# Order of small work beside a dense TensorE stream: key sums, kv, h split and query products, in linear attention with a gated feed-forward layer

## The chip, the cores and the metric

The kernel runs on one core of a Trainium2 chip. The metric is the device time of one execution in microseconds, the median of several runs. The engines are named as the profile names them: PE (TensorE matmuls), PEld (its weight loads), DVE (VectorE), ACT (ScalarE), POOL (GpSimd) and SP (SyncE, which here only issues DMAs).

## The reference

Linear attention over 8 batches, 8 heads, 576 tokens and 64 columns, then a gated feed-forward layer over all 4608 tokens:

```python
q_s = softmax(q, axis=-1)             # over the 64 columns
k_s = softmax(k, axis=2)              # over the 576 tokens
kv  = einsum('bhsd,bhse->bhde', k_s, v)
x   = einsum('bhsd,bhde->bhse', q_s, kv)      # then (4608, 512)
gate = sigmoid(x @ w_gate)            # (512, 1536)
out  = (gate * (x @ w_val)) @ w_out   # (1536, 512)
```

## The kernel before

**Blocks and steps.** The 4608 tokens are worked through in 9 blocks w of T = 512 (NW = 9). A block has NS = 6 steps, `at` 0 to 5; a step takes two of the twelve slices of 128 columns of the hidden width. Block 0 has code of its own beside the preparation of the weights, and its 12 slices are done by about 180 us. From block 1 on the main loop (lines 1061 to 1083) writes each step's work in one fixed order; each engine executes its own part of it in that order.

**A step.** `g1` (line 651) multiplies the block's x by w_gate and w_val in a Strassen-like scheme of seven products, each of 12 matmuls with 256 columns (L661), into three PSUM tiles y, z, rr. All operands are split into a high and a low fp32r part, and a product is hi x hi + hi x lo + lo x hi. Every product's result is moved to the SBUF tile `sg` by ACT (L679, L681, L684, L689) or added to it by DVE (L687, L693); ACT takes the sigmoids (L694, L697, L698), DVE multiplies gate and value (L700 to L702). The first product goes to y, the second to z, and the third adds to y, so it can't start before L679 has copied y away. `h_split` (line 706) then makes the high and low parts of h from `sg` on DVE (L711, L712). `g2` (line 720) multiplies the h of the step before by w_out in 24 matmuls of 512 columns (L729), so it lags g1 by one step. In step 0 that closes the block before, and `acc_out` copies its four results with ACT (L635) and sends them.

**The next block beside it.** `side_a` and `side_b` put the attention of block w + 1 into the steps of block w; `load_next` fetches what block w + 2 needs. By step:

- 0: DVE takes the maxima of q (natural layout) and subtracts them; the first two key tiles have their maxima subtracted.
- 1: the other three key tiles; ACT takes exp of q (L461), of the five key tiles (L361) and the last two of the four key sums (`k_sum`, L317: an exp over transposed keys whose sum is kept); DVE sums q.
- 2: PE multiplies keys by values (`k_mm`, L382, 40 matmuls of 128 columns); DVE subtracts the maxima from the transposed q (`qT_sub`, L493), which needs the qT and q_b transfers; `k_done` then divides kv by the key sums on DVE (L392) and splits it (ACT L416, DVE L417).
- 3 and 4: exp, scaling and split of the transposed q.
- 4: `x_mm` (line 532) multiplies q by kv (L542), and `x_ev` moves the result; `c_subs` builds Strassen sums, into ring tiles.
- 5: after g1, `c_split` splits the seven operands that the next block's g1 takes (ACT L600, DVE L601), then h_split follows. Their order is B11, T1, T2, B21, T3, B22, T4, which is also the order in which g1's products use them.

Batches of 576 and blocks of 512 don't match: a block of queries mostly has two parts that belong to two batches (`x_parts`), of 128 and 384 columns for block 2, then 192 and 320, 256 and 256, 320 and 192, 384 and 128, 448 and 64; block 8 has one part. `x_mm` multiplies each part by hi x hi, hi x lo and lo x hi of its batch's kv.

All transfers of q, k and v stand in SP's queue in program order. The `ring` pool of 11 buffers holds q and key tiles, the splits of q and the sums of c_subs in turn.

Of the kernel before, what the change touches and what calls it, by code (L numbers as in the profile page):

```python
# [21 lines left out]
T = 512  # L22
# [6 lines left out]
NS = NJ // 2  # L29
# [23 lines left out]
def attn_moe(ctx: ExitStack, tc: tile.TileContext, qf, qn, qT, k, kT, v, wg, wv, wo, out):  # L53
# [28 lines left out]
    kv_sb = const.tile([P, 2, 2, NP, P], F32R, name="kv_sb")  # L82
# [232 lines left out]
    def k_sum(b, hp):  # L315
        t = kT_sb.pop((b, hp))
        nc.scalar.activation(  # L317
            t, t, AF.Exp, bias=kneg[b][:, hp:hp + 1], accum_out=ksum[b][:, hp:hp + 1]
        )
# [33 lines left out]
    def k_sub(b, t, eng=nc.vector):  # L353
        n = KTILES[t][1]
        kt = kt_sb[b, t]
        eng.tensor_tensor(out=kt[:n], in0=kt[:n], in1=kmb[b][:n], op=ALU.subtract)

    def k_exp(b, t):
        n = KTILES[t][1]
        kt = kt_sb[b, t]  # L360
        nc.scalar.activation(kt[:n], kt[:n], AF.Exp)  # L361
# [13 lines left out]
    def k_mm(b, t):  # L375
        n = KTILES[t][1]
        kt, vt = kt_sb[b, t], v_sb[b, t]
        if t == 0:
            kvps[b] = ps_at.tile([P, NP, P], F32, name="at")
        for hp in range(NP):  # L380
            sl = slice(hp * P, (hp + 1) * P)
            nc.tensor.matmul(  # L382
                kvps[b][:, hp], lhsT=kt[:n, sl], rhs=vt[:n, sl],
                start=(t == 0 and hp == 0), stop=(t == len(KTILES) - 1 and hp == NP - 1),
                skip_group_check=True,
            )

    def diag_put(o, ps, k_r, h0, h1):

        for a in range(2):  # L390
            sl = slice(a * D, (a + 1) * D)
            nc.vector.tensor_tensor(  # L392
                out=o(sl), in0=ps[sl, :, sl],
                in1=k_r[sl, h0:h1].unsqueeze(2).broadcast_to([D, h1 - h0, D]), op=ALU.mult,
            )
# [8 lines left out]
    def k_done(b):  # L404
        k_r = ksum.pop(b)
        nc.vector.tensor_scalar_add(k_r, k_r, EPS)
        nc.vector.reciprocal(k_r, k_r)
        kv = kmax_b[:, 0:NP * D].rearrange("p (h e) -> p h e", e=D)
        diag_put(lambda sl: kv[sl], kvps.pop(b), k_r, 0, NP)
        kv_split(b, lambda sl: kv[sl])  # L410

    def kv_split(b, kv):
        hi, lo = (kv_sb[:, b % 2, i] for i in range(2))
        for a in range(2):
            sl = slice(a * D, (a + 1) * D)
            nc.scalar.copy(out=hi[sl, :, sl], in_=kv(sl))  # L416
            nc.vector.tensor_tensor(  # L417
                out=lo[sl, :, sl], in0=kv(sl), in1=hi[sl, :, sl].bitcast(F32), op=ALU.subtract
            )
# [19 lines left out]
    def qn_send(w, what):  # L439
        t = (q_m if what == "m" else q_r)[w]  # L440
        row = dpool.tile([H * T], F32, name=f"q_{what}_row")
        nc.sync.dma_start(
            out=row.rearrange("(p i) -> p i", p=P), in_=t.rearrange("p i one -> p (i one)")
        )
        q_row[w, what] = row.rearrange("(h t) -> h t", t=T)

    def qn_max(w, c):
        if c == 0:
            q_m[w] = const.tile([P, NC * TI, 1], F32, name="q_m")
        nc.vector.tensor_reduce(  # L450
            out=q_m[w][:, c * TI:(c + 1) * TI], in_=qn_sb[w, c], axis=AX.X, op=ALU.max
        )

    def qn_sub(w, c, eng=nc.vector):
        t = qn_sb[w, c]
        m = q_m[w][:, c * TI:(c + 1) * TI]
        eng.tensor_tensor(out=t, in0=t, in1=m.broadcast_to([P, TI, D]), op=ALU.subtract)

    def qn_exp(w, c):
        t = qn_sb[w, c]  # L460
        nc.scalar.activation(t, t, AF.Exp)  # L461
# [29 lines left out]
    def qT_sub(w, hp, eng=nc.vector):  # L491
        t = qT_sb[w, hp]
        eng.tensor_tensor(out=t, in0=t, in1=q_b.pop((w, "m", hp)), op=ALU.subtract)  # L493
# [12 lines left out]
    def qT_exp(w, hp):  # L506
        t = qT_sb[w, hp]
        nc.scalar.activation(t, t, AF.Exp)
# [15 lines left out]
    def x_parts(w):  # L524
        t0 = w * T
        b0, b1 = t0 // S, (t0 + T - 1) // S
        if b0 == b1:
            return [(b0, 0, T)]
        cut = b1 * S - t0
        return [(b0, 0, cut), (b1, cut, T)]  # L530

    def x_mm(w, hp):
        qh, ql = qT_hl.pop((w, hp))
        if w > 1 and hp < 3:
            ps = ps_gv.tile([P, T], F32, name="gv")
        else:
            ps = ps_at.tile([P, T], F32, name="at")
        x_ps[w, hp] = ps
        for b, f, t in x_parts(w):
            kh, kl = (kv_sb[:, b % 2, i, hp] for i in range(2))  # L540
            for lh, rh in ((0, qh), (0, ql), (1, qh)):
                nc.tensor.matmul(  # L542
                    ps[:, f:t], lhsT=kl if lh else kh, rhs=rh[:, f:t],
                    start=(lh == 0 and rh is qh), stop=(lh == 1),
                )

    def x_ev(w, hp):
# [26 lines left out]
    def quarter(kh, th):  # L574
        return x_32[:, 2 * kh:2 * kh + 2, th * HT:(th + 1) * HT]
# [15 lines left out]
    def c_split(i):  # L591
        if i == B11:
            t = bpool.tile([P, 1, 2, 2, HT], F32R, name="c_hl", tag="b")
            c_hl[i] = t[:, 0]
        elif i in C_PAIRS:
            t = cpool.tile([P, 2, 2, 2, HT], F32R, name="c_hl", tag=f"c{list(C_PAIRS).index(i)}")
            c_hl[i], c_hl[C_PAIRS[i]] = t[:, 0], t[:, 1]
        src = c_32.pop(i) if i in c_32 else quarter(*{B11: (0, 0), B21: (1, 0), B22: (1, 1)}[i])
        hi, lo = (c_hl[i][:, x] for x in range(2))
        nc.scalar.copy(out=hi, in_=src)  # L600
        nc.vector.tensor_tensor(out=lo, in0=src, in1=hi.bitcast(F32), op=ALU.subtract)  # L601
# [104 lines left out]
    def h_split(w, p):  # L706
        h_hl[w, p] = hi, lo = [
            two.tile([P, 2, T], F32R, name="h", tag=f"h_{x}") for x in ("hi", "lo")
        ]
        hi, lo = (t.rearrange("p i (q t) -> p (i q) t", q=2) for t in (hi, lo))  # L710
        nc.vector.tensor_copy(out=hi, in_=sg[:, :, 0])  # L711
        nc.vector.tensor_tensor(  # L712
            out=lo, in0=sg[:, :, 0], in1=hi.bitcast(F32), op=ALU.subtract
        )


    def step(w, i):
        return (i - 1) % NS if w == 1 else i
# [20 lines left out]
    def side_a(n, p):  # L739

        b = n if n < B else None
        if p == 0:
            for c in range(NC):
                qn_max(n, c)
            qn_send(n, "m")
            for c in range(NC):
                qn_sub(n, c)
            if b is not None:
                k_sub(b, 0); k_sub(b, 1)
        if p == 1:  # L750
            if b is not None:
                for t in range(2, 5):
                    k_sub(b, t)
            for c in range(NC):
                qn_exp(n, c)
            if b is not None:
                for t in range(5):
                    k_exp(b, t)
                k_sum(b, 2); k_sum(b, 3)
            for c in range(NC):  # L760
                qn_sum(n, c)
        if p == 2:
            if b is not None:
                for t in range(5):
                    k_mm(b, t)
            for hp in range(NP):
                qT_sub(n, hp)
            if b is not None:
                k_done(b)
        if p == 3:  # L770
            for hp in range(NP):
                qT_exp(n, hp)
        if p == 4:
            for hp in range(NP):
                qT_split(n, hp)
# [57 lines left out]
    def after_first(j):  # L833
# [28 lines left out]
        if 6 <= j <= 9:  # L862
            x_mm(1, j - 6)
# [76 lines left out]
    ps = ps_acc.tile([P, DM], F32, name="acc")  # L940
# [116 lines left out]
    def wo_next(w, at):  # L1057
        wo_load(w, step(w, at))

    prev = None  # L1060
    for w in range(1, NW):
        last = w == NW - 1
        for at in range(NS):
            p = step(w, at)
            end = last and at == NS - 1
            g1(w, p, None if end else step(w + (at + 1) // NS, (at + 1) % NS))
            if at == NS - 1 and not last:
                for i in range(7):
                    c_split(i)
            h_split(w, p)  # L1070
            if not last:
                side_a(w + 1, at)
            if prev is None:
                g2_0(NJ - 1)
                wo_next(1, 0)
                wo_next(1, 1)
            else:
                g2(*prev)
                if not end:
                    wo_next(w + (at + 1) // NS, (at + 1) % NS)  # L1080
            prev = (w, at)
            if not last:
                side_b(w + 1, at)
# [39 lines left out]
```

## Time and profile before

| | us |
|---|---|
| median of three runs | 983.6 |
| the other runs | 982.94, 3356.91 |
| the profiled execution | 980.61 |
| its span, first to last instruction | 978.8 |

The profile is of one execution. Times in it count from the span's start. A product of PE overlaps the next one's, so rows give it a duration (0.28 us for 256 columns) longer than the distance between two of them. In the timeline a number in brackets is how long the engine sat idle before the row, and what ended that.

### The profile page before, as it was taken

What the parts mean: (1) busy time and instruction counts of PE and PEld (TensorE: products, weight loads), DVE (VectorE), ACT (ScalarE), POOL (GpSimd) and SP (SyncE); (2) the same over time, 40 slices, a digit from 0 to 9 for tenths busy, and PEclk for the clock granted to TensorE, in tenths of its full rate; (3) what the DMA queues carried; (4) which work ended last, traced back from release to release, by engine and by line L of the source; (5) the groups of instructions that cost most, each with busy time, mean ns of one, the idle gap of its engine ahead of it and who ended that gap; (6) DMA issues with size and microseconds to landing.
All of it is one profiled execution on the core that took longest, in us unless ns stands there. A gap on an engine that the chain in (4) does not pass through costs nothing.

```text
span 978.8 us, 15635 instructions
## 1 busy us (share of the span) xinstructions
PE 947.4 (97%) x6062; PEld 817.1 (83%) x6062; DVE 612.9 (63%) x1013; ACT 471.5 (48%) x812; POOL 167.2 (17%) x316
## 2 busy tenths in 40 slices
PE   5899998999999999999999999999999999999998
PEld 4444543799999999999989999899998999999997
DVE  7788878766566666656675568457644656473242
ACT  4689784563446343625462545253434434443222
POOL 0110001221112111211211111121212121212210
PEclk7999999899999999999999999999999999999999
DMA  9976475899699968997899779997998779868672
GB/s 330 342 273 254 185 274 205 288 350 317 200 269 340 312 203 251 353 296 248 207 379 300 245 160 373 316 270 143 364 315 238 215 238 313 241 181 258 200 215 77
DMA packets 93864, 257.78 MB, mean 263 GB/s; under 512 B 15264, under 2 KB 17568, under 8 KB 93024
## 3 DMA queue, kind: packets, MB, share of 16 engines
q0 software_dynamic: 43712, 168.32, 57.0%
q1 hardware_dynamic: 50080, 88.48, 31.0%
q8 instruction: 48, 0.79, 0.4%
q14 instruction: 24, 0.20, 0.1%
HBM read 228.20 MB, written 28.56 MB: 262 GB/s over the span
## 4 chain that ended last, share of the span: by engine, by line
PE 62%; DMA 20%; issue 6%; DVE 5%; ACT 5%; SPq 1%; POOL 0%; DVEq 0%; POOLq 0%; ACTq 0%
PE gv L661 38%; PE acc L729 20%; DMA ring<-k_in 5%; DMA q_m_row<-q_m 4%; DMA q_b<-q_m_row 3%; DMA ring<-qT_in 2%; PE gv L542 2%; PE at L382 1%; DMA wo_raw<-wo_in 1%; DMA ring<-qf_in 1%; PE acc L643 1%; DMA sg<-wv_in 1%; DMA lent<-v_in 1%; DMA out<-x 1%; ACT ring L461 1%
## 5 line engine op out<-in xcount | busy, mean ns | idle before, releaser
L661 PE MATMUL gv<-c_hl,s_sb 128*128 128x256 f32 x2304 | 286.6, 279 | 5.6 <-ACT sg L679 5.5
L661 PEld LDWEIGHTS gv<-c_hl,s_sb 128*128 128x128 f32 x2304 | 275.2, 188 | 8.2 <-ACT sg L679 7.8
L729 PE MATMUL acc<-wo_hl,h 128*128 128x512 f32 x1152 | 272.2, 392 | 0.0
L729 PEld LDWEIGHTS acc<-wo_hl,h 128*128 128x128 f32 x1152 | 212.9, 188 | 44.4
L661 PE MATMUL gv<-c_hl,a_w 128*128 128x256 f32 x1728 | 224.6, 279 | 0.0
L661 PEld LDWEIGHTS gv<-c_hl,a_w 128*128 128x128 f32 x1728 | 213.8, 188 | 4.3 <-issue 1.0
L282 POOL DMA_DIRECT2D s_sb<-s x188 | 100.1, 532 | 321.0 <-PE gv L661 320.0
L687 DVE TENSOR_TENSOR sg<-gv,sg 128x512 f32<-128x512 f32 x48 | 33.2, 692 | 161.4 <-PE gv L661 161.4
L238 POOL DMA_DIRECT2D wo_hl<-wo x96 | 50.9, 531 | 297.3 <-PE acc L729 297.2
L689 ACT COPY sg<-gv 128x512 f32<-128x512 f32 x48 | 28.1, 586 | 105.5 <-PE gv L661 105.5
L616 PE MATMUL gv<-x,f_w 128*128 128x512 f32 x160 | 72.4, 606 | 3.6 <-ACT h L624 3.5
L679 ACT COPY sg<-gv 128x512 f32<-128x512 f32 x48 | 28.0, 583 | 88.8 <-PE gv L661 64.5
L691 DVE TENSOR_TENSOR sg<-sg 128x512 f32<-128x512 f32 x48 | 33.2, 693 | 59.6 <-ACT sg L689 59.6
L616 PEld LDWEIGHTS gv<-x,f_w 128*128 128x128 f32 x160 | 30.5, 194 | 41.9 <-issue 36.0
L712 DVE TENSOR_TENSOR h<-sg,h 128x1024 fp32r<-128x1024 f32 x48 | 58.8, 1226 | 1.6
L694 ACT ACTIVATE sg<-sg 128x512 f32<-128x512 f32 x48 | 30.4, 633 | 55.3 <-DVE sg L693 55.3
L700 DVE TENSOR_TENSOR sg<-sg 128x512 f32<-128x512 f32 x48 | 33.2, 692 | 33.5 <-ACT sg L694 33.5
L643 PE MATMUL acc<-wo_t,h 128*128 128x512 f32 x96 | 45.8, 622 | 5.6 <-DVE h L628 5.6
L684 ACT COPY sg<-gv 128x512 f32<-128x512 f32 x48 | 28.1, 586 | 44.2 <-PE gv L661 44.2
L643 PEld LDWEIGHTS acc<-wo_t,h 128*128 128x128 f32 x96 | 19.0, 200 | 30.1 <-issue 22.4
L681 ACT COPY sg<-gv 128x512 f32<-128x512 f32 x48 | 28.1, 586 | 25.5 <-PE gv L661 25.4
L416 ACT CAST kv_sb<-kmax_b 64x256 fp32r<-64x256 f32 x14 | 5.7, 404 | 69.1 <-DVE kmax_b L392 68.8
(152 smaller groups left out, 1046.4 us busy)
## 6 DMA issues: line engine op xcount, KB each, us to landing
s_sb<-s POOLq DMA_DIRECT2D x188, 512.0 KB, 7.3
wo_hl<-wo POOLq DMA_DIRECT2D x96, 512.0 KB, 6.2
s<-s_sb POOLq DMA_DIRECT2D x6, 2048.0 KB, 7.6
out<-x SPq DMA_DIRECT2D x36, 256.0 KB, 10.0
ring<-k_in SPq DMA_DIRECT2D x28, 256.0 KB, 14.0
ring<-qn_in SPq DMA_DIRECT2D x28, 256.0 KB, 9.8
q_b<-q_m_row SPq DMA_DIRECT2D x56, 128.0 KB, 8.9
ring<-qT_in SPq DMA_DIRECT2D x28, 256.0 KB, 9.1
```

The source lines that it names most:

```text
L238: nc.gpsimd.dma_start(out=t.rearrange("p h e -> p (h e)"), in_=wo_dram[2 * p + i].bitcast(F32R))
L282: nc.gpsimd.dma_start(out=s_sb[:, i].rearrange("p h n e -> p (h n e)"), in_=s_dram[p][:, i * n:(i + 1) * n].bitcast(F32R),)
L616: nc.tensor.matmul(ps[n], lhsT=w[:, kt // 2, sl], rhs=x_0[:, kt], start=(kt == 0), stop=(kt == NK - 1),)
L643: nc.tensor.matmul(acc[0][m], lhsT=h_0[j][:, m * P:(m + 1) * P], rhs=wo_t[j // 2][:, j % 2], start=(j == 0), stop=(j == NJ - 1),)
L661: nc.tensor.matmul(ps[:, n], lhsT=lh(kt), rhs=c_hl[i][:, x, kt], start=(first and n == 0 and kt == 0 and lh is wh and x == 0), stop=(last ...
L681: nc.scalar.copy(out=sg[:, 2], in_=z)
L687: nc.vector.tensor_tensor(out=sg[:, 0], in0=rr, in1=sg[:, 0], op=ALU.add)
L691: nc.vector.tensor_tensor(out=sg[:, 3], in0=sg[:, 3], in1=sg[:, 2], op=ALU.add)
L694: nc.scalar.activation(sg[:, 0:2, 0], sg[:, 0:2, 0], AF.Sigmoid)
L700: tt(out=sg[:, 0:2, 0], in0=sg[:, 0:2, 0], in1=sg[:, 0:2, 1], op=ALU.mult)
L712: nc.vector.tensor_tensor(out=lo, in0=sg[:, :, 0], in1=hi.bitcast(F32), op=ALU.subtract)
L729: nc.tensor.matmul(acc[w][m], lhsT=h[lh][:, i, sl], rhs=o[i][:, rh], start=(at == 0 and i == 0 and lh == 0 and rh == 0), stop=(at == NS - ...
```

## The change

- `x_mm` goes through the three products outermost and the block's parts innermost, so matmuls of the two parts alternate; the first matmul alone has the start flag, the last alone the stop flag.
- `side_a`: the last two key sums move from step 1 to step 0. `k_done` moves ahead of the four `qT_sub` in step 2.
- The main loop's last step splits three operands of the next block, then h, then the other four, in place of all seven and then h.

```diff
--- before.py
+++ after.py
@@ -536,12 +536,13 @@
         else:
             ps = ps_at.tile([P, T], F32, name="at")
         x_ps[w, hp] = ps
-        for b, f, t in x_parts(w):
-            kh, kl = (kv_sb[:, b % 2, i, hp] for i in range(2))
-            for lh, rh in ((0, qh), (0, ql), (1, qh)):
+        parts = x_parts(w)
+        for lh, rh in ((0, qh), (0, ql), (1, qh)):
+            for b, f, t in parts:
                 nc.tensor.matmul(
-                    ps[:, f:t], lhsT=kl if lh else kh, rhs=rh[:, f:t],
-                    start=(lh == 0 and rh is qh), stop=(lh == 1),
+                    ps[:, f:t], lhsT=kv_sb[:, b % 2, lh, hp], rhs=rh[:, f:t],
+                    start=(lh == 0 and rh is qh and f == 0), stop=(lh == 1 and t == T),
+                    skip_group_check=True,
                 )
 
     def x_ev(w, hp):
@@ -747,6 +748,7 @@
                 qn_sub(n, c)
             if b is not None:
                 k_sub(b, 0); k_sub(b, 1)
+                k_sum(b, 2); k_sum(b, 3)
         if p == 1:
             if b is not None:
                 for t in range(2, 5):
@@ -756,17 +758,15 @@
             if b is not None:
                 for t in range(5):
                     k_exp(b, t)
-                k_sum(b, 2); k_sum(b, 3)
             for c in range(NC):
                 qn_sum(n, c)
         if p == 2:
             if b is not None:
                 for t in range(5):
                     k_mm(b, t)
+                k_done(b)
             for hp in range(NP):
                 qT_sub(n, hp)
-            if b is not None:
-                k_done(b)
         if p == 3:
             for hp in range(NP):
                 qT_exp(n, hp)
@@ -1064,10 +1064,13 @@
             p = step(w, at)
             end = last and at == NS - 1
             g1(w, p, None if end else step(w + (at + 1) // NS, (at + 1) % NS))
-            if at == NS - 1 and not last:
-                for i in range(7):
+            ahead = 3 if at == NS - 1 and not last else 0
+            for i in range(ahead):
+                c_split(i)
+            h_split(w, p)
+            if ahead:
+                for i in range(ahead, 7):
                     c_split(i)
-            h_split(w, p)
             if not last:
                 side_a(w + 1, at)
             if prev is None:
```

## Rows read from the trace of the kernel before

**Rows 1.** the page: PE's busy time, share, instructions; granted clock by 40 slices

```profile
PE 947.4 (97%) x6062; PEld 817.1 (83%) x6062; DVE 612.9 (63%) x1013; ACT 471.5 (48%) x812; POOL 167.2 (17%) x316
...
PEclk7999999899999999999999999999999999999999
```

**Rows 2.** groups by line (busy, mean ns, idle before); waits (total, times, longest)

```profile
L661 PEld LDWEIGHTS gv<-c_hl,s_sb 128*128 128x128 f32 x2304 | 275.2, 188 | 8.2 <-ACT sg L679 7.8
...
PEld gv L661 <- ACT sg L679: 7.8, 11, 1.5
```

**Rows 3.** timeline, block 4, step 2 (start, us, engine, line, [idle before <- releaser])

```profile
508.47 1.52 PE L661 MATMUL gv<-c_hl,a_w 128*128 128x256 f32 x12
...
509.77 0.76 ACT L317 ACTIVATE kt<-kt,k_neg 128x576 f32<-128x576 f32 x1
...
511.29 0.56 ACT L679 COPY sg<-gv 128x512 f32<-128x512 f32 x1
...
511.90 1.24 PEld L661 LDWEIGHTS gv<-c_hl,s_sb 128*128 128x128 f32 x10 [0.75 <-ACT sg L679]
...
511.90 1.68 PE L661 MATMUL gv<-c_hl,s_sb 128*128 128x256 f32 x12 [0.55 <-ACT sg L679]
```

**Rows 4.** timeline, block 6, steps 2 to 4: DVE, ACT and the weight loads

```profile
731.85 2.53 DVE L493 TENSOR_TENSOR ring<-ring,q_b 128x512 f32<-128x512 f32 x4 [6.26 <-DMA ring<-qT_in]
...
739.95 0.69 DVE L687 TENSOR_TENSOR sg<-gv,sg 128x512 f32<-128x512 f32 x1 [3.40 <-PE gv L661]
...
735.22 0.86 ACT L416 CAST kv_sb<-kmax_b 64x256 fp32r<-64x256 f32 x2 [12.44 <-DVE kmax_b L392]
...
750.98 0.58 ACT L679 COPY sg<-gv 128x512 f32<-128x512 f32 x1 [2.84 <-PE gv L661]
...
736.74 1.36 PEld L661 LDWEIGHTS gv<-c_hl,s_sb 128*128 128x128 f32 x11 [1.54 <-ACT sg L679]
```

**Rows 5.** timeline, block 2, step 0: two c splits of DVE, ACT's copy

```profile
274.36 1.29 DVE L601 TENSOR_TENSOR c_hl<-ring,c_hl 128x512 fp32r<-128x512 f32 x2
...
280.01 0.59 ACT L679 COPY sg<-gv 128x512 f32<-128x512 f32 x1 [3.35 <-DVE h L712]
```

**Rows 6.** timeline of ACT, block 2, step 0; group of L694's table loads

```profile
287.34 0.63 ACT L694 ACTIVATE sg<-sg 128x512 f32<-128x512 f32 x1 [1.55 <-DVE sg L693]
...
291.47 2.65 ACT L635 COPY x<-acc 128x512 f32<-128x512 f32 x4 [2.93 <-PE acc L729]
...
L694 ACT ACT_TABLE_LOAD x14 | 18.0, 1283 | 0.2
```

**Rows 7.** timeline of ACT, block 1, steps 0 and 1

```profile
190.06 0.58 ACT L635 COPY x<-acc 128x512 f32<-128x512 f32 x1 [0.34 <-PE acc L643]
...
194.04 0.58 ACT L679 COPY sg<-gv 128x512 f32<-128x512 f32 x1 [0.83 <-PE gv L661]
```

**Rows 8.** L542 alone in stretches (stretch, length, PE busy), then two products' timeline row

```profile
258.98:262.41 3.43, 3.43 (x24) 3.27 (x23) 1.00 0.70 228
...
764.44:768.10 3.66, 3.66 (x24) 3.50 (x23) 1.00 0.79 261
sum 16.67, PE 16.67 PEld 16.24; mean PE 3.33 PEld 3.25
...
460.42:463.14 2.72, 2.72 (x24) 2.68 (x23) 1.00 0.64 191
...
258.98 0.33 PE L542 MATMUL gv<-ring,kv_sb 128*128 128x128 f32 x2
```

**Rows 9.** chain of waits (start, us, what): whole g1 and g2 steps

```profile
863.54 9.89 PE gv L661 x84
873.44 5.49 PE acc L729 x24
878.93 10.03 PE gv L661 x84
...
894.47 9.52 PE gv L661 x84
```

## The prediction

> **What bounds the kernel now.** I read the page's busy shares first: PE is busy for 97% of the span, and after the start its granted clock is at the upper of its two levels, 2.4 GHz, in every slice [rows 1]. So time can only come from PE's own idle time, from the pace of its products, or from fewer of them; the change leaves their number alone. The table of the groups by line, weight loads apart, then says where PE idles: before the loads of L661 that read c_hl and s_sb it sat 8.2 us, 7.8 of them until ACT's copy at L679; no DMA ends a wait of PE there [rows 2]. The view of the waits counts 11 of these of some size, up to 1.5 us [rows 2]. Why L679: g1's third product adds into the same PSUM tile y that L679 copies, so if ACT is late PE has two products (24 matmuls) of grace and then stands.
>
> Three kinds of lateness show in the timeline.
>
> *Step 2 of a block.* ACT leaves step 1 with an exp table load of 1.28 us, four exps of q, five of k and two key sums (L317); only at 511.29 does L679 start, and PE waits: 0.75 us at the weight loads, and the twelve matmuls after it last 1.68 us, where the twelve at the step's start lasted 1.52: over 0.1 more, as the pipeline fills anew [rows 3]. There are six such waits, one a block, of 0.59 to 0.75, about 4.1 us; the rows show the first with 0.75.
>
> *Step 3.* DVE stands for the qT transfer (6.26 us), then does the four subtractions, and only then k_done; ACT's L416, in front of L679 in its queue, waits 12.44 us for that, and PE 1.54 us [rows 4]. Four steps show this, 0.13 to 1.54 us, about 3.4 us; the rows show the longest.
>
> *Step 0.* Seven splits and the two operations of h_split stand in DVE's queue; L679 may overwrite sg only when L712 is done, so it starts at 280.01 after 3.35 us of idle time, and PE loses a little [rows 5]. Seven small ones, 0.7 us.
>
> 4.1 + 3.4 + 0.7 = 8.2, the whole of the group's idle time. With 0.1 us of refilling for each of the 11 waits the price is 9.3 us.
>
> **The change part by part.**
>
> *Key sums a step sooner.* Removes 1.52 us from ACT's queue in front of L679 in step 2 (509.77 to 511.29). L679 then could start at 509.77; its product ends about 510.0 (g1 starts at 508.47, twelve matmuls take 1.36 and the copy follows some 0.2 later), so ACT is done at 510.6, where PE wants y at 511.19. The wait goes with 0.6 us to spare. What is added: the sums now stand in step 0, after sigmoids, so they need an exp table load there, 1.28 us, and the sigmoids of step 1 need theirs back. The first costs nothing in blocks 2 to 6: ACT sits idle 2.93 us before L635, and 1.28 + 1.52 = 2.80 [rows 3, 6]. Without that cover it would push L635 and then L679 of step 1. The second falls in the 1.55 us in which L694 waits for DVE [rows 6]; so do the 14 loads under L694 now, in other steps. In the first block the cover is thin: 0.34 us of idle before the first of four copies, about as much before each other, and 0.83 before L679 [rows 7], some 2 in all where 2.80 come in. L679 would end up to 0.8 us later, and PE has the second product, 1.4 us, of grace. I charge 0.2 us; ends are 0 and 0.8. The earlier sums also free kt a step sooner for the two kT transfers, which helps SP if anything.
>
> *kv finished first.* The four subtractions and k_done change places on DVE. L392 waits for the key products of PE, which stand a whole g2 (5.49 us, [rows 9]) ahead of step 3's g1, and needs no transfer, so L416 is done some 4 us before that g1 begins, and L679 waits for its product alone. The 3.4 us go. What is late next: where qT landed early, the subtractions stand behind the wait for PE, at most about 3 us later than now, and with them the release of q_b for the second four transfers. Behind them on DVE stand two maxima and then L687, which now waits 3.40 us for PE in the example [rows 4]; with PE 1.5 us earlier there is 1.9 left. I cost it at nothing.
>
> *h split among the c splits.* The same nine DVE operations; four splits of DVE, two of which take 1.29 us, pass behind h, so L712 ends 2.4 us sooner, near 277.5, and L679 waits for its product instead [rows 5]. B21, the first split that moves back, ends near 278.2 and is needed by the fourth product, 36 matmuls (4.1 us) into a g1 that starts near 277.8. The 0.7 us go. T3 and T4 end 1.9 us later and with them their two ring buffers, into which keys may be loaded; see the rivals.
>
> *Long and short query products alternate.* Same matmuls. A block's 24 take 2.72 us where its parts are equal, 256 and 256; the five uneven ones take 16.67 [rows 8], 3.1 over 5 x 2.72. From 256 and 512 columns, 0.113 and 0.229 us each (2.72 / 24, and 5.49 / 24 in g2 [rows 9]), a line gives 0.171 for 384; twelve take 2.05 of the first block's 3.43, so a short one of 128 costs 0.115 where the line says 0.055. So it is in the last: 448 gives 0.200, and a 64 takes (3.66 - 2.40) / 12 = 0.105. Three shorts in a row each wait for their weights. The first short behind a long one does not: by 259.05 two products of 128 columns had started, the first at 258.98 [rows 8]. In the new order every short follows a long one. Bounds: nothing, if the long one behind then waits as long, and 3.1 if all loads hide. I take 2.4: a short of 64 or 128 at 0.06, one of 192 at 0.09 (the line says 0.084), which saves 0.7, 0.3, 0.3, 0.6 and 0.5 in the five blocks, since the row shows the very pattern.
>
> *The pace of the 256-column products.* Not an edit, but the wait's removal touches it. With no wait, g1 takes either 9.52 us (0.113 a matmul) or 9.89 (0.118), at the same clock [rows 9]. Of those whole in the chain 11 have the first, 16 the second; scaled to 48 steps, 20 and 28. It stays over many steps and changes only where PE meets other products or a wait: long after uneven query products (all five), short again after some waits, as after the last block's first step, 10.03 with a small wait after seven long ones and then five of 9.52 (the rows show the last long one and the first short one) [rows 9]. That wait goes. Bounds: all short, 28 x 0.37 = -10.4 us; all long, 20 x 0.37 = +7.4. I take the last block staying long: 5 x 0.37 = +1.9.
>
> **Sum.** -9.3 + 0.2 - 2.4 + 1.9 = -9.6 us. The profiled execution took 980.61 us (span 978.8) and would take 971.0; the median of the runs is 3.0 higher, so 983.6 - 9.6 = 974.0.
>
> **A rule that speaks against it.** The rows price a table load at 1.28 us with 0.2 us of idle in 14 of them [rows 6]. The Trainium skill, "ScalarE: Activation LUTs", asks in its section "Table sets: the hidden batching unit" to do all work of one set before changing, and in "What ACT_TABLE_LOAD costs" puts a change at about 2.66 us, 1.38 of it a drain; the key sums now leave the batch of exps. By that figure step 1's sigmoids would slip 2.66 - 1.55 = 1.1 us, 0.5 more than there is to spare in step 2, in six blocks, and the sum would be -6.6 rather than -9.6. The sum goes by the rows.
>
> **Rivals.**
> 1. *The waits move.* L694 of step 1 comes late by a table load that doesn't hide, and step 1's exps start as much later: the 0.6 us to spare in step 2 are gone and its waits come back. Against it: a load under L694 is on the path in no row. Only 3.4 + 0.7 + five tenths of refilling and 2.4 are gained; the 0.2 and the 1.9 stay: 983.6 - 4.9 = 978.7. By that rule of the Trainium skill it would come so. Chance 0.12.
> 2. *All long pace:* 983.6 - 9.3 + 0.2 - 2.4 + 7.4 = 979.5. For it: nothing but chance disturbs the pace once the waits are gone. Chance 0.12.
> 3. *All short pace:* 983.6 - 11.5 - 10.4 = 961.7, over 2% faster. For it: the last block kept it for five steps [rows 9]. Chance 0.07.
> 4. *Slower: the query transfers.* SP's queue is one file: k loads into the ring, maxima of q, their spreading, qT. In the example DVE waits 6.26 us for qT [rows 4]. If keys wait for T4's buffer, all shift by 1.9 us. L687 has 1.9 us to give, as above, and L679 of step 4, which must find h read, stood 2.84 us idle for PE [rows 4]: below some 5 us of delay nothing shows, above it each us costs PE one in six blocks. From 5 + 9.6/6 = 6.6 us on the kernel is slower than before; at 8 it is 983.6 - 9.6 + 18 = 992. Against it: the change adds 1.9. Chance 0.04.
> That alternating gains nothing is within my case: 976.4.
>
> **How the numbers follow.** My case has 0.65, with its own range 969 to 979 (the 2.4 and the 1.9 at their ends, and half of the runs' 3 us). To leave out no more than two in ten I take rivals 1 and 2 in: 967 to 981. What can be told from no change here is about 2%, 19.7 us: faster (below 963.9) is most of rival 3, 0.05; slower (above 1003) the tail of rival 4, 0.02; within 2%: 0.93.
>
> **What would show it.** Idle before L661's loads on L679 near zero in steps 0, 2 and 3; else that step was wrong. L416 waiting under 6 us, L317 with a table load in step 0 of six blocks, and L694 with 20 loads and its wait for DVE still there. The five uneven blocks of L542 near 14.3 us. The count of 9.52 and 9.89 tells the pace; if the waits are gone and the time is off, that is where I was wrong.

## The result, and the profile after

The changed kernel takes 974.35 us (median; 973.67 to 974.96), the one before 983.27 in the same comparison: a ratio of 0.9919, 95% interval 0.9889 to 0.9948. Measured once more beside e5 and e6 it was 974.42 against 979.97, 0.9941 (0.9922 to 0.9961). One run of before, of 3356.91 us, counts in the median of 983.27, and in the 983.6 from which the forecast starts, but not in the ratio; without it before's median is 982.94. The forecast was 974.0. It was right for the total, and two of its steps, the alternation of the query products and the distance between the profiled execution and the median, were still wrong; so the parts matter more than the sum. The profiled execution took 974.62 us, its span 972.9 (980.61 and 978.8 before).

In code after line 539 the lines are one further on than before: L661 is now L662, L679 L680, L694 L695, L635 L636, L729 L730. L317, L392, L416, L493 and L542 have kept theirs.

The page of after, busy time and granted clock:

```profile
PE 948.6 (98%) x6062; PEld 821.0 (84%) x6062; DVE 613.3 (63%) x1013; ACT 488.6 (50%) x824; POOL 169.7 (17%) x316
...
PEclk8899999899999999999999999999999999999999
```

The same matmuls at the same clock as in [rows 1], and ACT has 12 instructions more: the table loads. The groups by line of after (busy, mean ns | idle before):

```profile
L662 PEld LDWEIGHTS gv<-c_hl,s_sb 128*128 128x128 f32 x2304 | 275.0, 188 | 0.0
...
L695 ACT ACT_TABLE_LOAD x20 | 25.7, 1283 | 0.4
...
L317 ACT ACT_TABLE_LOAD x7 | 9.0, 1283 | 0.1
```

The 8.2 us that PE's weight loads stood before this group [rows 2] are 0.0. Where the time went can be summed from the starts of PE's matmuls, each to the start of the next; from the first g1 of block 1 to the end of the span:

| us | before | after | difference |
|---|---|---|---|
| start to the first g1 of block 1 | 178.70 | 180.28 | +1.6 |
| g1 of all steps | 477.91 | 470.28 | -7.6 |
| of this, waits and the refilling after them | 10.56 | 0.99 | -9.6 |
| of this, pace (2770 matmuls of 256 columns at the slower one, 2334 before; 4.4 ns each) | | | +1.9 |
| query products (L542) | 22.15 | 22.28 | +0.1 |
| g2, key products, the rest | 300.1 | 300.0 | -0.1 |
| span | 978.8 | 972.9 | -6.0 |

The distances of the g1 row are shared out between waits and pace by stretches, which is sure to some 0.2 us. In the code of the first row the change touches the query products of block 1 alone, and these take 5.39 us before and 5.40 after. In the other profiles below the first g1 starts at 178.2 to 180.7 us, whichever kernel it is, so 1.6 is scatter.

### The profile page after: what moved, and what is told of

It is laid out like the page before. It is cut to its first block, busy times and chain, and to the rows that moved or that the text cites. A ratio compares the mean times of both kernels' runs of the same rounds, so it can differ in the third digit from the quotient of the medians.

```text
span 972.9 us, 15630 instructions
## 1 busy us (share of the span) xinstructions
PE 948.6 (98%) x6062; PEld 821.0 (84%) x6062; DVE 613.3 (63%) x1013; ACT 488.6 (50%) x824; POOL 169.7 (17%) x316
## 4 chain that ended last, share of the span: by engine, by line
PE 82%; DMA 6%; issue 5%; DVE 4%; ACT 2%; POOL 0%; SPq 0%; POOLq 0%; ACTq 0%; DVEq 0%
PE gv L662 48%; PE acc L730 27%; PE at L382 3%; PE gv L542 2%; DMA lent<-v_in 1%; DMA wo_raw<-wo_in 1%; PE acc L644 1%; DMA lent<-kT_in 1%; DMA ring<-qf_in 1%; DMA s<-s_sb 1%; PE at L542 1%; DMA lent<-k_in 1%; DVE s L250 1%; DVE s_sb L273 0%; DVE a_w L273 0%
## 5 line engine op out<-in xcount | busy, mean ns | idle before, releaser
L662 PE MATMUL gv<-c_hl,s_sb 128*128 128x256 f32 x2304 | 283.7, 278 | 0.0
L662 PEld LDWEIGHTS gv<-c_hl,s_sb 128*128 128x128 f32 x2304 | 275.0, 188 | 0.0
L730 PE MATMUL acc<-wo_hl,h 128*128 128x512 f32 x1152 | 272.3, 392 | 0.0
L730 PEld LDWEIGHTS acc<-wo_hl,h 128*128 128x128 f32 x1152 | 213.0, 188 | 44.5
L662 PE MATMUL gv<-c_hl,a_w 128*128 128x256 f32 x1728 | 225.5, 279 | 0.0
L662 PEld LDWEIGHTS gv<-c_hl,a_w 128*128 128x128 f32 x1728 | 214.5, 188 | 4.3 <-issue 1.0
L688 DVE TENSOR_TENSOR sg<-gv,sg 128x512 f32<-128x512 f32 x48 | 33.2, 691 | 162.0 <-PE gv L662 161.8
L680 ACT COPY sg<-gv 128x512 f32<-128x512 f32 x48 | 28.2, 588 | 120.4 <-PE gv L662 118.7
L695 ACT ACTIVATE sg<-sg 128x512 f32<-128x512 f32 x48 | 30.4, 633 | 47.7 <-DVE sg L694 47.7
L644 PEld LDWEIGHTS acc<-wo_t,h 128*128 128x128 f32 x96 | 19.2, 202 | 30.1 <-issue 22.2
L694 DVE TENSOR_TENSOR sg<-gv,sg 128x512 f32<-128x512 f32 x48 | 33.2, 692 | 4.1
```

Of the source, the lines that this page charges most:

```text
L644: nc.tensor.matmul(acc[0][m], lhsT=h_0[j][:, m * P:(m + 1) * P], rhs=wo_t[j // 2][:, j % 2], start=(j == 0), stop=(j == NJ - 1),)
L662: nc.tensor.matmul(ps[:, n], lhsT=lh(kt), rhs=c_hl[i][:, x, kt], start=(first and n == 0 and kt == 0 and lh is wh and x == 0), stop=(last ...
L688: nc.vector.tensor_tensor(out=sg[:, 0], in0=rr, in1=sg[:, 0], op=ALU.add)
L694: nc.vector.tensor_tensor(out=sg[:, 1], in0=z, in1=sg[:, 1], op=ALU.add)
L695: nc.scalar.activation(sg[:, 0:2, 0], sg[:, 0:2, 0], AF.Sigmoid)
L730: nc.tensor.matmul(acc[w][m], lhsT=h[lh][:, i, sl], rhs=o[i][:, rh], start=(at == 0 and i == 0 and lh == 0 and rh == 0), stop=(at == NS - ...
```

## Experiments

| | kernel | us | before beside it | ratio (95%) |
|---|---|---|---|---|
| e1 | the change with the old query products | 974.33 | 978.98 | 0.9941 (0.9921 to 0.9961) |
| e2 | before, key sums sooner, alone | 978.44 | 978.98 | 0.9989 (0.9971 to 1.0007) |
| e3 | before, kv first, alone | 980.36 | 978.98 | 1.0003 (0.9981 to 1.0026) |
| e4 | before, h among the splits, alone | 981.85 | 978.98 | 1.0018 (0.9990 to 1.0046) |
| e5 | the change, with halves after the key products | 974.05, one run | 979.97 | |
| e6 | the same, with the pace led at more places | 966.48 | 979.97 | 0.9858 (0.9832 to 0.9883) |
| e7 | the change again | 974.42 | 979.97 | 0.9941 (0.9922 to 0.9961) |
| e8 | e6 with other places | 965.21 | 981.91 | 0.9830 (0.9812 to 0.9848) |
| e9 | the change, short query products halved | 974.92, one run | 981.91 | |

### e1: the change without the alternation

```diff
-        parts = x_parts(w)
-        for lh, rh in ((0, qh), (0, ql), (1, qh)):
-            for b, f, t in parts:
+        for b, f, t in x_parts(w):
+            kh, kl = (kv_sb[:, b % 2, i, hp] for i in range(2))
+            for lh, rh in ((0, qh), (0, ql), (1, qh)):
...
```

> The changed kernel, with the query products in the old order (the three products of one part, then of the other). Theory A, a load floor: in either order each short product brings some 0.11 us, the time of the weight load that can't run under it, so the five uneven blocks of L542 take 16.7 us in both orders and the kernel stays within 0.3% of the changed one, apart from the pace in which it leaves these blocks. Rival: the first-short row was right and something else took the gain back; then the old order shows the same 16.7 us, but the new order's long products would wait for something that the old order's do not, such as a PSUM tile, with a releaser in the waits. The equal block is 2.72 us if it is entered at the short pace and 2.83 at the long, in either order.

The whole time is that of the change (974.33 beside 974.35 and 974.42). L542 alone in stretches (stretch, length, PE busy), the first and the last of the five uneven blocks and the sum of the five, after:

```profile
260.10:263.54 3.44, 3.44 (x24) 3.34 (x23) 1.00 0.71 229
...
756.91:760.65 3.74, 3.73 (x24) 3.51 (x23) 1.00 0.83 250
sum 16.71, PE 16.70 PEld 16.21; mean PE 3.34 PEld 3.24
```

and e1, the same two blocks:

```profile
260.82:264.26 3.44, 3.44 (x24) 3.28 (x23) 1.00 0.67 225
758.66:762.33 3.67, 3.67 (x24) 3.51 (x23) 1.00 0.88 285
```

Before had 3.43, 3.66 and a sum of 16.67 [rows 8]; e1's five sum to 16.70. The order of long and short is worth nothing. From the start of a matmul to the start of the next (its columns, then ns), the first block's products begin as follows:

```
before  128: 57   128: 114  128: 111  384: 229  384: 169  384: 170
after   128: 61   384: 226  128: 61   384: 225  128: 61   384: 226
```

In the old order the first short one is over in 57 ns, as I read it in the row, but the first long one then takes 229 where the other two take 170. In the new order every long one does: a pair takes 0.287 us, about as much as the 0.111 of a short one that waits for its weights and the 0.170 of a long one. With 192 and 320 columns a pair takes 0.256, with 64 and 448 it takes 0.311, again close to the old sums. The starts of the weight loads (PEld) in this stretch of after tell it more plainly: 260.10, 260.21, 260.39, 260.49 and 260.67 us, so 0.11 and 0.18 in turn, and the first, third and fifth start together with a short product. The load that starts with a short product outlasts it, whatever stands ahead of that product.

### e9: is it the weight load of each product?

If so, more products of fewer columns must cost about 0.11 us each, though the columns are the same. e9 makes every short part (under 256 columns, from block 2 on) as two halves, 12 matmuls more in each of the five blocks:

```diff
+        parts = [
+            (b, f + c * (t - f) // n, f + (c + 1) * (t - f) // n)
+            for b, f, t in parts for n in [2 if t - f < 256 and w > 1 else 1] for c in range(n)
+        ]
```

> The changed kernel; in blocks 2 to 7 each query product of under 256 columns is made as two of half its columns: as many columns, 12 more matmuls and weight loads in each of five uneven blocks. Theory A, every load that a short product brings costs its own 0.11 us whatever its columns: the five uneven blocks go from 16.7 to 16.7 + 5 x 12 x 0.11 = 23.3 us, the equal block stays at 2.7 to 2.8, and the kernel takes some 6.6 us more, the pace aside. Rival, products cost by columns and the new order's long ones wait for something else: 16.7 to 17.5.

The same lines of e9, in its five uneven blocks, the first of them and the sum:

```profile
257.78:262.58 4.80, 4.80 (x36) 4.70 (x35) 1.00 0.49 160
...
sum 23.31, PE 23.30 PEld 22.95; mean PE 4.66 PEld 4.59
```

23.31 - 16.71 = 6.6 us for 60 matmuls more, 0.11 each, though the columns are the same: short products have a least cost, which no order hides. That this is the weight load fits the starts above; but every matmul of this kernel has a load of its own, so no run parts the load from another fixed cost of a matmul. The whole time of this one run (974.92) doesn't show the 6.6 us: its g1 steps happened to run at the slower pace in 21 of 48 cases where after has 33, 12 x 0.37 = 4.4 us back, and its first g1 starts 1.9 us sooner (178.35). The pace is what e5 to e8 are about.

### e2, e3, e4: the three edits for the waits, each alone

Each is before with one hunk of the diff above: the two lines of `k_sum` (e2), `k_done` ahead of `qT_sub` (e3), the main loop's last step (e4).

> The kernel before, with the key sums a step sooner alone. Theory A, each part takes its own waits: the six idle times of PE's weight loads in step 2 (4.1 us) go, those of step 0 (0.7) stay, those of step 3 stay or grow, since the query transfers land at the same time and PE comes 0.8 us earlier: 3.4 to 7 us. Time 2 to 5 us less, the pace aside. Rival B, the table load is on the path: waits of step 2 stay at 0.3 us or more each, and L694 of step 1 no longer waits for DVE.

> The kernel before, with kv finished ahead of the query subtractions alone. Theory A: the idle times of step 3 (3.4 us) go, those of step 2 (4.1) and step 0 (0.7) stay; ACT's L416 waits under 6 us. Time about 3.5 us less, the pace aside. Rival B: step 3's wait was the transfer's and moves to the subtractions' readers; then idle time of PE remains in step 3 or 4.

> The kernel before, with h split among the c splits alone. Theory A: the seven small idle times of step 0 (0.7 us) go and the others stay at 7.5 us or a little more; time within 1 us of the kernel before, the pace aside. Rival B: the later splits hold ring buffers, the key loads come 1.9 us later and step 3's waits grow by 1 to 4 us.

The views of the waits, PE's weight loads on ACT's copy L679 (total, times, longest), where before had 7.8, 11, 1.5 [rows 2]; first e2, then e3, then e4:

```profile
PEld gv L661 <- ACT sg L679: 4.7, 6, 1.7
```

```profile
PEld gv L661 <- ACT sg L679: 4.5, 8, 0.7
```

```profile
PEld gv L661 <- ACT sg L679: 3.7, 6, 0.7
```

By steps: e2 has none left in step 2 and keeps steps 3 (0.30 to 1.66, 4.3 us in all) and 0. e3 has none left in step 3, and keeps six in step 2 (4.1 us) and those of step 0. e4 has none left in step 0 and keeps six in step 2 (3.7 us). Each edit takes away its own kind of wait and leaves the others, as forecast. One thing doesn't fit: in e4 step 3 has only one wait, of 0.08 us, though nothing was done about it. There the transfers of the transposed q came earlier (DVE's L493 waited 22.2 us for them, 29.6 before). Step 3's waits hang on when transfers land; in the profiles with the old order they come to 0.1, 3.4 and 4.3 us.

None of the three alone gives a time that differs surely from before's. One reason shows in the profiles: the pace of g1 takes back a good part of the gains, in e4 more than all. Counted by matmuls, 28 of before's 48 g1 steps run at the slower pace, 32 of e2's, 33 of e3's and 46 of e4's. In the g1 of these profiles waits and refilling cost 3.5, 3.3 and 5.2 us less than before's, the pace 1.5, 1.6 and 6.5 us more.

### e5, e6, e8: what sets the pace of g1

The chain of waits of after (start, us, what) has whole steps; this is the key products of step 2 and the steps around them in blocks 2 and 3:

```profile
309.90 9.89 PE gv L662 x84
319.79 4.66 PE at L382 x40
324.45 5.72 PE acc L730 x24
330.17 9.52 PE gv L662 x84
...
408.32 9.52 PE gv L662 x84
417.84 4.66 PE at L382 x40
422.49 5.71 PE acc L730 x24
428.20 9.89 PE gv L662 x84
```

A g1 takes 9.89 or 9.52 us, and it changes over at the key products: from long to short in block 2, from short to long in block 3. In after it goes from short to long four times of four (blocks 1, 3, 5, 6), and from long to short twice (2, 4); in e1 it also stays long, twice. The starts of the matmuls say by what: in g2 the distances run 226, 229 and 232 ns in turn, and the g1 behind it takes 113.3 ns a matmul if g2's last distance (from its last matmul to g1's first) was 231 or 232, and 117.7 if it was 225 to 230. In the eleven profiles of this document 407 g1 steps follow a g2 that ends on whole matmuls, 187 of them short and 220 long, and none goes against this. A g2 has 24 matmuls, eight whole turns, so a short pace lives on until something with another count or another pattern comes between: across a g2 alone it stayed short 135 times of 135, and across key products and a g2 it turned long 17 times of 17. A long pace is less sure: across a g2 alone it stayed long 186 times and turned short 37 times, and why is open.

If that is the cause, two matmuls more or fewer in a g2 choose the pace. In e5 the last two of the 24 are made as two halves each, in the g2 after the key products; columns and sums are the same, and four times 0.113 is as long as two times 0.229 us:

```diff
+HALVED = {(w, 1): 2 for w in range(1, 7)}
...
+                for n, (lh, rh) in enumerate(((0, 0), (0, 1), (1, 0))):
+                    cut = 2 if i == 1 and m == NT - 1 and n >= 3 - HALVED.get((w, at), 0) else 1
+                    for c in range(cut):
+                        cs = slice(c * DM // cut, (c + 1) * DM // cut)
+                        nc.tensor.matmul(acc[w][m][:, cs], lhsT=h[lh][:, i, sl], rhs=o[i][:, rh, cs],
...
```

> The changed kernel; in the g2 that follows the key products of blocks 1 to 6, the last two matmuls of 512 columns are each made as two of 256 (same columns, same result; two more weight loads). Theory P, the pace of the 256-column products is a phase that PE carries along: within g2 the distances run 226, 229, 232 ns in turn, and the pace after it is short if the last distance is 231 or 232, long if it is 226 or 229. In the changed kernel's trace a g2 after key products that were entered short ends on 229, and 232 comes two matmuls earlier; so halving the last two leaves steps 3 and 4 short where step 2 was short (blocks 3 to 6, and 1 if its step 2 is short), and turns those of block 2, entered long, to long. Blocks 4, 5 and 6 then are short but for step 5: about 23 long g1 of 48 where the changed kernel has 31. Rival: the pace is chance, or depends on the transfers beside it; then the count stays near 31 and the short ones lie anywhere.

It missed: 36 long steps, not 23, and 974.05 us. The rule itself held, in blocks 4 and 5: where step 2 was short, the halves kept steps 3 and 4 short. But where step 2 was long, in blocks 1, 2, 3 and 6, the same halves left step 3 long (block 3 turned short only in step 4, across a g2 without halves). What they undo is the key products' shift, so the pace must be short before them. e6 therefore halves two in one g2 ahead of that as well, in block 1's step 5, and one in block 6's (the diff is against e5):

```diff
-HALVED = {(w, 1): 2 for w in range(1, 7)}
+HALVED = {**{(w, 1): 2 for w in range(1, 7)}, (1, 4): 2, (6, 4): 1}
```

> As the run before, and also the last two matmuls halved in the g2 of step 5 in block 1 (its query products leave a distance of 229 last) and the last one halved in the g2 of step 5 in block 6 (226 last, 232 one matmul earlier). By theory P everything from block 2 on is short but for step 5 of blocks 4 to 6: 7 to 9 long g1 of 48, some 23 fewer than in the changed kernel, 8 to 9 us less: about 0.991 of the changed kernel and 0.98 to 0.985 of the kernel before. Rival, chance: no difference beyond 2 us from the changed kernel.

966.48 us, 14 long steps where 7 to 9 were expected: blocks 2 to 5 did as they should, block 6 was entered with 229 as g2's last distance and so ran long. e8 mends that place, and leaves block 1's keys alone (against e6):

```diff
-HALVED = {**{(w, 1): 2 for w in range(1, 7)}, (1, 4): 2, (6, 4): 1}
+HALVED = {**{(w, 1): 2 for w in range(2, 7)}, (1, 4): 2, (5, 4): 2, (6, 4): 1}
```

> As the run before with the led pace, but with two matmuls halved in the g2 of step 5 in block 5 too (in that run it ended on 229, 231 came two matmuls earlier, and block 6 stayed long for it), and none in block 1's step 2, which was entered long there and left long through the halves. By theory P blocks 2 to 6 are short but for their step 5; block 1's steps 3 and 4 too, if its step 2 was long. Blocks 7 and 8 depend on how the products of 448 and 64 columns leave PE when entered short, which no run has shown: short if one halved matmul is right, long otherwise. 8 to 10 long g1 of 48 and 963 to 966 us in the first case, 20 and 968 in the second. Rival, chance: 30 long and 974.

965.21 us with 9 long steps. The chain of waits of e8, block 4's key products (L383 here; its g2 has 26 matmuls, two pairs of which are halves) and the last g1 of the kernel:

```profile
504.64 9.52 PE gv L663 x84
514.17 4.66 PE at L383 x40
518.82 5.71 PE acc L734 x26
524.53 9.52 PE gv L663 x84
...
939.23 9.52 PE gv L663 x84
```

Short stays short across the keys, where after turns long. In e5, e6 and e8 together it stayed short in all 11 places where the halves met a short pace, and long in all 6 where they met a long one. One place of e8 wasn't led: block 7's first step ran long in spite of the matmul halved by `(6, 4)`, and its second turned short across a g2 without halves. The gain fits the count: 33 - 9 = 24 steps of 0.37 us are 8.9 us, and the medians (of two comparisons) are 974.4 - 965.2 = 9.2 apart; beside the kernel before, the ratios are 0.9830 and 0.9941. In the profiles the g1 take 470.3 and 462.5 us, 7.8 apart, since e8's first one holds a wait of 1.16 us for DVE. e8 beats both kernels, at the same number of columns and nearly the same granted clock (0.989 over the whole span, 0.987 in after).

### e7: the change again

> The changed kernel itself, for the same chip and runs as the two above. By theory P its pattern of paces after block 1 is the same as in its first profile: long in blocks 7 and 8, short in steps 3 to 5 of block 2 and 0 to 2 of block 3, and so on: 31 long give or take the first block's. By chance, another pattern. Ratio to the kernel before 0.990 to 0.997, since that kernel's waits in step 3 differ from run to run by up to 3 us.

974.42 us. From block 1's query products on, its long and short steps stand in the same places as in the first profile of after: 32 long steps, 33 there. With no wait in the way the pace repeated, in these two profiles.

## Why the forecast came true, point by point

**The waits (-9.3): right, -9.6.** Key sums: the timeline of ACT, the steps in question, shows each wait gone for the reason given. Block 4, steps 1 and 2, after:

```profile
500.34 1.28 ACT L695 ACT_TABLE_LOAD   x1
501.88 0.63 ACT L695 ACTIVATE sg<-sg 128x512 f32<-128x512 f32 x1 [0.25 <-DVE sg L694]
...
506.50 2.70 ACT L361 ACTIVATE ring<-ring 128x512 f32<-128x512 f32 x5
509.48 0.59 ACT L680 COPY sg<-gv 128x512 f32<-128x512 f32 x1 [0.28 <-PE gv L662]
```

No key sum stands between the exps (L361) and the copy, so ACT waits for PE's product (0.28 us) where PE waited 0.75 for the copy [rows 3]. kv first, block 6, DVE and then ACT:

```profile
720.61 0.88 DVE L392 TENSOR_TENSOR kmax_b<-at,k_sum 64x256 f32<-64x256 f32 x2 [0.99 <-PE at L382]
...
725.18 2.71 DVE L493 TENSOR_TENSOR ring<-ring,q_b 128x512 f32<-128x512 f32 x4 [2.79 <-DMA ring<-qT_in]
732.04 0.69 DVE L688 TENSOR_TENSOR sg<-gv,sg 128x512 f32<-128x512 f32 x1 [4.15 <-PE gv L662]
...
721.06 0.86 ACT L416 CAST kv_sb<-kmax_b 64x256 fp32r<-64x256 f32 x2 [4.54 <-DVE kmax_b L392]
727.73 0.59 ACT L680 COPY sg<-gv 128x512 f32<-128x512 f32 x1 [5.81 <-PE gv L662]
```

L392 waits for the key products alone, L416 waits 4.54 us where it was 12.44 [rows 4], and DVE still stands for the transfer, behind kv, where it stops nobody. h among the splits, block 2, step 0:

```profile
277.41 1.23 DVE L713 TENSOR_TENSOR h<-sg,h 128x1024 fp32r<-128x1024 f32 x1
...
280.55 0.59 ACT L680 COPY sg<-gv 128x512 f32<-128x512 f32 x1 [2.76 <-PE gv L662]
```

h is done at 278.64, where it was done just before 280.01 [rows 5], though the c splits start 1.1 us later in this profile, and the copy waits for PE. e2 to e4 show that each edit does this by itself.

**The first block (+0.2): 0.** ACT in block 1 after, the cover that I called thin:

```profile
194.14 2.02 ACT L636 COPY x<-acc 128x512 f32<-128x512 f32 x4
196.04 0.61 ACT L680 COPY sg<-gv 128x512 f32<-128x512 f32 x1
```

L680 ends at 196.65, 3.05 us after its g1's first matmul (193.60), with no idle time left before it; in before it ended at 194.62, 2.59 us after (192.03) [rows 7]. So it comes 0.46 us later, and PE has no wait for it: the grace of a product was enough.

**The table loads: hidden, and rival 1 fell.** ACT in block 2, steps 0 and 1, after:

```profile
289.57 1.28 ACT L317 ACT_TABLE_LOAD   x1
290.87 0.78 ACT L317 ACTIVATE kt<-kt,k_neg 128x576 f32<-128x576 f32 x1
...
292.48 2.65 ACT L636 COPY x<-acc 128x512 f32<-128x512 f32 x4
```

The load takes 1.28 us, and the next ACTIVATE starts 0.02 later; L636 comes a little late and nothing waits. L695 has 20 loads, and after the new one it still waits 0.25 us for DVE (above), where a step without a load shows 1.55 [rows 6]: 1.28 of the wait went to the load and none came through. The Trainium skill, "ScalarE: Activation LUTs", section "What ACT_TABLE_LOAD costs", puts a change of set at about 2.66 us, 1.38 of it a drain; the trace agrees with the other 1.28, the load itself, but not with the drain: none stands between the load and the ACTIVATE behind it, nor ahead of the load. The rule to batch the work of one set, in its section "Table sets: the hidden batching unit", makes no exception for loads that fill a wait; here 12 loads more, 15.4 us of ACT, cost PE nothing.

**The query transfers (rival 4)** didn't come late: the waits of DVE, L493 for qT, are shorter than before's; before's line, then after's:

```profile
DVE ring L493 <- DMA ring<-qT_in: 29.6, 10, 6.3
DVE ring L493 <- DMA ring<-qT_in: 13.4, 9, 2.8
```

Some of that is only that kv's wait now comes ahead of it; whether the transfers are earlier too is not separated.

**The alternation (-2.4): wrong, +0.1.** The failed step is the reading of one row. From the start of the second short product at 0.06 us [rows 8] I took it that the first had cost 0.06. A product's start says only when the product ahead has let it in; the weights that weren't ready are paid for by the next distance, the 229 ns of the first long one in the same stretch. The row that could have told is the sum: 3.43 us is close to three times 0.111 + 0.170, four times over (3.37), without any short one for nothing. The lower bound that I gave, "nothing, if the long one behind then waits as long", is what happened.

**The pace (+1.9): +1.9, by the right place.** The last block ran all six g1 steps at 9.89, as forecast when its small wait goes; the others shuffled and came out even. That they did was luck, and I couldn't have known it: e7, the same kernel, has one long step fewer, e1 four more; and the five uneven query products no longer all leave it long (363.28 us has 9.52 behind the second). Rivals 2 and 3 were the ends of a thing that e8 shows can, for the most part, be set by hand.

**The total** came out right with two errors that cancel. For the profiled execution I expected 971.0 and it took 974.62: 2.5 us from the alternation and 1.6 from the code ahead of the main loop, less 0.3 and 0.2 from waits and first block. To get the median I added before's 3.0 us between median and profiled execution; after has no such distance (974.35 and 974.62). So the hit is partly luck. The forecast starts from 983.6, a high median of three runs, the 3356.91 among them; in the later comparisons before's median is 978.98, 979.97 and 981.91. The forecast ratio, 974.0 to 983.6 or 0.990, lies inside the interval of the first comparison (0.9889 to 0.9948) and outside that of the second (0.9922 to 0.9961). Before spreads over 976.5 to 984.4 us in all its other runs, after over 972.8 to 977.2. The waits of step 3, which vary with the transfers, and the pace, which follows the waits, are likely sources of that spread; runs without a profile don't show it, so this stays argued. It also would explain why the gain was 9 us in one comparison and 5.6 in the next.

## What to carry to other kernels

A wait of the bound engine goes away if what stands ahead of its releaser in that engine's queue is moved to where the engine has time to spare, and three such moves add up; each was visible in the views of the groups, the waits and one timeline window. A matmul's start in a stream isn't its cost: cost a pattern by the length of its whole repeat, and try the sum both ways before you credit a saving. Where a stream of equal matmuls has two lengths of step at one clock, look at what came before it, since a fill-in of the same columns in other pieces can choose the shorter one.

## What the runs showed of the hardware

**Two paces at one clock.** Matmuls of 256 columns with a weight load each run at 113.3 or 117.7 ns from start to start, at a granted clock of 1.00 in both; which of the two goes with the phase of a turn of three distances (226, 229, 232 ns) that the 512-column matmuls ahead of them left behind, in 407 of 407 cases. Another count of them, 22 whole ones and four halves in place of 24, kept the short pace across key products, where it otherwise turned long (11 of 11 places, against 0 of 17 without). The short pace can hold for whole blocks (block 8 of e8). In this kernel it is worth 0.37 us a step and, from e8, 9 us of 974. What in the engine makes the turn of three is open; no run here tells.

**A matmul with a weight load of its own has a least cost.** With 64, 128 or 192 columns, in order or alternating with long ones, and in e9 with 32, 64 or 96, each costs about 0.11 us, the distance at which loads of 128 x 128 follow each other (e1, e9); no longer neighbour hides it. That it is the load that sets this is argued from the starts of the loads, not parted from other fixed costs.
